# Moving weight splits, prepared sums and decoding units between VectorE and GpSimd in a planned attention and expert kernel

## The chip, the cores and the metric

The kernel runs on one core of a Trainium2 chip. Its time is the device time of one execution in microseconds (us). A core has TensorE (PE in the profile; its weight loads are PEld), VectorE (DVE), ScalarE (ACT), GpSimd (POOL) and SyncE (SP), which here issues every DMA. Each engine works through its own instructions strictly in the order of the program and waits on semaphores for the others. DVE, ACT and POOL work on SBUF; matmuls write PSUM, which DVE and ACT read.

## The reference

Three layers follow one another; only shapes and formulas matter here.

```
attention: B,H,S,D = 2,8,768,64; state = gamma[h]*state + k_t v_t ; y_t = scale * q_t state
experts:   x = attention as (1536, 512); P = softmax-like weights (1536, 8), 8 rounds of row and column scaling
           out = sum over e of P[:, e] * (relu(x @ w1[e]) @ w2[e]),   w1 (8,512,1024), w2 (8,1024,512)
last:      h = x @ w_in (512,2048); g = max(h,0) + alpha*min(h,0); out = g @ w_out (2048,512)
```

w_in, w_out and alpha come in as 64-bit numbers; the kernel turns w_in and w_out into 32-bit ones itself ("decoding").

## The kernel before

After the attention (the first 64 us) the work is 20 phases. Phases 0 to 7 are the eight experts on batch 0, phases 8 to 15 the same experts on batch 1 ("fast" in the code), phases 16 to 19 the last layer, two for each batch. A phase takes four weight units j = 0 to 3; weight unit n is 4 x phase + j.

**Split numbers.** Each 32-bit operand is split into a high part, rounded by ACT, and a low part, the difference, made by DVE or POOL. A product is three matmuls (high x high, high x low, low x high; lines 195 to 197).

**Layer 1** uses seven products of half blocks for each unit (Strassen-Winograd), six matmuls of 384 columns each. The list `order` has the 28 products of a phase; places 0 to 27 below mean "after that product". Unit 3 has its products (3,1), (3,5), (3,6), (3,2), (3,7) at places 19, 20, 22, 24 and 25, with products of unit 2 at 21 and 23. After product 6 DVE adds PSUM tile B and tile d into tile E (L700), and product 7 then goes on accumulating in B. So PE may not start product 7 of a unit before DVE has read B. For unit 0 there is one product between 6 and 7 (places 2 and 4), for the others there are two (8 and 11, 15 and 18, 22 and 25). After product 7 DVE adds again (L713, tile D). DVE makes the low halves hl of the layer's output (L656).

**Layer 2** of phases 0 to 7 and 16 to 19 is plain: six token tiles t0 to t5, 24 matmuls of 512 columns each; places 28 to 39 are t0a, t0, t1a, ... t5 (half a tile each). In phases 8 to 15 it is seven-product work again, 28 steps u at places 28 to 55, with weight pieces that phases 0 to 7 prepared and stored in DRAM (c2).

**Work beside the products** is put by hand at places, by `step(ph, pos, fn)`; what stands at one place goes to each engine in the order of registration:
- w1 units (L106 sums, L126 high, L135 low; tiles raw0, wa, wb, wc).
- w2 high (L145) and low (L150; tiles raw1, v). In phases 1 to 7 units 0 and 1 have their low part on DVE, units 2 and 3 on POOL, each in one instruction of 1024 columns.
- "prepared" units (`prep_at`: load, four sums L177, high L181, two low halves L185, two stores; tiles pr, pw): five a phase in phases 1 to 6, two in phase 7. The sums of one a phase are on DVE, of the others on POOL.
- decoding units (`decode_at`: load, `bits` = L593, L595, L598 on DVE, `power` = L603 on ACT, `join` = L609, L612 on DVE, store and the next load): 32 in all, 18 before phase 8 and two in each of phases 8 to 14. The load of the next unit is issued with the store of the last, into one buffer.
- in phases 10 to 15, `gather` (L826 on POOL) adds the eight weighted tiles t of the phase before to the total.

Of the kernel before, what the change touches and what calls it, by code (L numbers as in the profile page):

```python
# [44 lines left out]
def tile_kernel(ctx, tc, qkT, kv, ctab, w_gate, w1, w2, w_in, w_out, alpha, out):  # L45
# [31 lines left out]
    def w_load(kind, n):  # L77
        if n >= NJ * len(PHASES) or (kind, n) in raw:
            return
        ph, j = divmod(n, NJ)  # L80
        _, e = PHASES[ph]
        if kind == 1 and ph in FAST:
            return
        width = (1792, 1024)[kind]
        t = (stg, pools["raw1"])[kind].tile([128, width], F32, tag=f"raw{kind}", name=f"raw{kind}_{n}")
        src = (w1, w2)[kind][NJ * e + j] if e < E else wd[kind][NJ * (e - E) + j]
        if ph in FAST:
            nc.sync.dma_start(out=t[:, 0:768], in_=src[:, 0:768])
# [73 lines left out]
    def prep_load(i):  # L162
        if i >= NJ * E:
            return
        q = 2 if i == NJ * E - 1 else i % 3
        pr[i] = (pools["prep"] if q == 2 else tmp).tile([128, 1024], F32, tag="u" + "abc"[q], name=f"pr{i}")
        nc.sync.dma_start(out=pr[i], in_=w2[i])

    def prep_sums(i, eng, part):
        s11, s21, s12, s22 = (pr[i][:, 256 * q:256 * q + 256] for q in range(4))  # L170
        for out, in0, in1, op in (
            (s22, s21, s22, ALU.add),
            (s21, s11, s21, ALU.subtract),
            (s11, s22, s11, ALU.subtract),
            (s12, s12, s11, ALU.subtract),
        )[part]:
            eng.tensor_tensor(out=out, in0=in0, in1=in1, op=op)  # L177
# [113 lines left out]
    with tc.manual_schedule():  # L291
# [605 lines left out]
        def at(ph, key, *fns):  # L897
            hooks.setdefault((ph, key), []).extend(fns)
# [41 lines left out]
        for ph in range(len(PHASES)):  # L940
            n = NJ * ph
            fast = ph in FAST
            eng = dve if fast else pool
            if 1 <= ph <= 6:
                if ph > 1:
                    decode_at(ph, 15, 17, 19, 21)
                for i in (30, 36):
                    decode_at(ph, i, i + 1, i + 2, i + 3)
                prep_at(ph, dve, 9, 13, 16, (20, 23), 26)
                for q in (25, 30, 33, 36):  # L950
                    h = max(q, 27)
                    prep_at(ph, pool, q, q, h + 2, (h + 3, h + 3), h + 4)
            elif ph == 7:
                decode_at(ph, 15, 17, 19, 21)
                prep_at(ph, dve, 9, 13, 16, (20, 23), 26)
                prep_at(ph, pool, 25, 25, 30, (31, 31), 33)
            if fast:
                w1_at(ph, n + 2, pool, dve, 0, 2, 3, 3, 5, 7, 9)
                w1_at(ph, n + 3, pool, dve, 5, 9, 11, 10, 12, 14, 16)
                w1_at(ph, n + 4, pool, dve, 36, 36, 38, 39, 40, 42, 43)  # L960
                w1_at(ph, n + 5, pool, dve, 44, 44, 45, 48, 49, 50, 52)
            else:
                w1_at(ph, n + 2, pool, pool, 0, 3, 3, 6, 6, 9, 9)
                w1_at(ph, n + 3, pool, pool, 5, 10, 10, 12, 12, 16, 16)
                if ph > 0:
                    w1_at(ph, n + 4, dve, dve, 29, 29, 30, 31, 32, 31, 32)
                    w1_at(ph, n + 5, dve, dve, 33, 33, 34, 35, 36, 35, 36)
                early = ((4, 6, dve), (9, 12, dve), (15, 16, pool), (20, 21, pool))
                usual = ((12, 12, pool), (17, 17, pool), (19, 19, pool), (23, 23, pool))
                for j, (hi, lo, eng) in enumerate(early if 0 < ph < E else usual):  # L970
                    step(ph, hi, lambda m=n + j: w2_high(m))
                    step(ph, lo, lambda m=n + j, eng=eng: w2_low(m, eng))
                if ph < E:
                    for j, pos in enumerate((19, 22, 29, 31)):
                        step(ph, pos, lambda m=n + j: w2_keep(m))
            if fast:
                if ph < 2 * E - 1:
                    decode_at(ph, 5, 7, *((8, 9) if ph == E else (9, 11)))
                    decode_at(ph, 19, 21, 23, 25)
                if ph > E + 1:  # L980
# [12 lines left out]
                if ph in (E + 1, E + 4):
                    step(ph, 0, lambda k=(ph - E - 1) // 3: xk.extend(x_keep(2, k)))
                if E < ph < 2 * E - 1:
                    for keys in ((12, 17, 18, 27), (37, 39, 41, 45), (46, 48, 50, 55)):
                        i = unit[0] - NJ * E
                        if i >= 7 * ((ph - E - 1) // 3 + 1):
                            continue
                        unit[0] += 1  # L1000
                        for q, pos in enumerate(keys):
                            step(ph, pos, lambda i=i, q=q: xk[i][q]())
            if ph + 1 in XGROUP:
                g = XGROUP[ph + 1]
# [139 lines left out]
```

## Time and profile before

| | us |
|---|---|
| median of 3 runs | 1328.22 (1328.04 to 1329.6) |
| the profiled execution's own time | 1330.52 |
| its span | 1328.7 |
| PE busy | 1289.4 (97%) |
| DVE busy | 958.7 (72%) |
| ACT busy | 634.7 (48%) |
| POOL busy | 518.9 (39%) |

The span is the time from the first to the last instruction; 1.8 us of the execution lie around it. A busy share is an average over stages with different limits; matmuls overlap one another, so a busy PE is not a PE at full rate. The groups below name a line of the kernel before, an engine, and tiles as output<-inputs.

### The profile page before, as it was taken

The numbers are of one execution on the slowest core, as the hardware profiler recorded it, in microseconds if no ns is written. First come the engines' busy times: TensorE is split into PE (matmuls) and PEld (weight loads), VectorE is DVE, ScalarE is ACT, GpSimd is POOL, SyncE is SP. The second block draws the span as 40 slices with busy tenths as digits, with TensorE's granted clock in tenths as the row PEclk, the third lists the DMA queues.
The fourth block names the chain that finished last, engine by engine and source line by source line (L and its number), as shares of the span: only waits on it lengthen the run. The fifth ranks groups of instructions, "written<-read, shape, count | busy, mean of one in ns | idle before, by whom it ended". The sixth has DMA issues, their size and how long they took to land.

```text
span 1328.7 us, 19564 instructions
## 1 busy us (share of the span) xinstructions
PE 1289.4 (97%) x7179; PEld 1195.4 (90%) x7179; DVE 958.7 (72%) x1462; ACT 634.7 (48%) x1129; POOL 518.9 (39%) x435
## 2 busy tenths in 40 slices
PE   9899999999898989899999999999999999999998
PEld 6798988888888888888999999999999998989897
DVE  5646787888888787965878878797886775586371
ACT  2452625252626252544455646455564654646370
POOL 4860656464747473700004040322402272525160
PEclk9999999999999999999999999999999999999999
DMA  9464798888888888976768586776857572243111
GB/s 362 169 200 146 225 298 292 282 296 292 284 304 298 282 297 278 313 243 216 242 211 300 190 278 210 268 237 226 295 171 253 178 273 82 68 137 105 55 32 48
DMA packets 152255, 296.80 MB, mean 223 GB/s; under 512 B 11952, under 2 KB 77024, under 8 KB 152160
## 3 DMA queue, kind: packets, MB, share of 16 engines
q1 hardware_dynamic: 152160, 295.57, 66.1%
q8 instruction: 56, 0.92, 0.3%
q14 instruction: 39, 0.32, 0.1%
HBM read 198.24 MB, written 97.28 MB: 222 GB/s over the span
## 4 chain that ended last, share of the span: by engine, by line
PE 69%; DVE 12%; DMA 5%; issue 5%; ACT 5%; POOL 2%; SPq 2%; DVEq 0%; ACTq 0%; POOLq 0%
PE o L195 7%; PE o L197 7%; PE o L196 7%; PE B L195 7%; PE B L197 7%; PE B L196 7%; PE A L195 4%; PE A L197 4%; PE A L196 4%; PE D L196 2%; PE D L195 2%; PE D L197 2%; PE E L196 2%; PE E L195 2%; PE E L197 2%
## 5 line engine op out<-in xcount | busy, mean ns | idle before, releaser
L177 POOL TENSOR_TENSOR pr<-pr 128x256 f32<-128x256 f32 x100 | 97.9, 979 | 138.7 <-DMA pr<-in_w_dram 113.3
L106 POOL TENSOR_TENSOR raw<-raw 128x256 f32<-128x256 f32 x108 | 95.1, 891 | 92.7 <-DMA raw<-in_w_dram 24.4
L784 ACT ACTIVATE hs<-b 128x768 fp32r<-128x768 f32 x112 | 93.9, 846 | 32.5 <-PE A L197 11.4
L826 POOL TENSOR_TENSOR total<-total,t 128x384 f32<-128x384 f32 x56 | 66.3, 1212 | 103.2 <-DVE t L822 103.1
L794 DVE TENSOR_TENSOR hs<-b,hs 128x768 fp32r<-128x768 f32 x96 | 92.6, 972 | 14.8 <-ACT hs L784 14.8
L700 DVE TENSOR_TENSOR E<-B,d 128x384 f32<-128x384 f32 x80 | 45.1, 563 | 69.3 <-PE B L197 64.3
L697 ACT ACTIVATE B<-A 128x384 f32<-128x384 f32 x80 | 38.8, 485 | 104.8 <-PE A L197 103.0
L259 POOL TENSOR_TENSOR xs<-b,xs 128x384 fp32r<-128x384 f32 x6 | 6.2, 1025 | 199.4 <-DMA rd<-in_w_in_dram 120.9
L181 ACT ACTIVATE pw<-pr 128x1024 fp32r<-128x1024 f32 x32 | 33.8, 1056 | 82.1 <-POOL pr L177 79.4
L197 PE MATMUL B<-hs,ws 128*128 128x384 f32 x192 | 64.2, 334 | 0.0
L195 PE MATMUL B<-hs,ws 128*128 128x384 f32 x192 | 64.1, 334 | 0.0
L196 PE MATMUL B<-hs,ws 128*128 128x384 f32 x192 | 64.1, 334 | 0.0
L748 DVE SCALAR_TENSOR_TENSOR total<-o,P,total 128x512 f32<-128x512 f32 x42 | 31.3, 746 | 42.9 <-PE o L197 42.9
L185 DVE TENSOR_TENSOR pr<-pr,pw 128x512 fp32r<-128x512 f32 x64 | 60.1, 971 | 0.0
L603 ACT ACTIVATE ex<-ex,ebias 128x512 uint32<-128x512 uint32 x32 | 23.0, 718 | 65.6 <-DVE ex L593 65.6
L106 DVE TENSOR_TENSOR raw<-raw 128x256 f32<-128x256 f32 x84 | 50.1, 614 | 1.9 <-DMA raw<-in_w_dram 0.5
L713 DVE TENSOR_TENSOR D<-B,d 128x384 f32<-128x384 f32 x48 | 26.9, 561 | 23.2 <-PE B L197 23.1
L742 ACT ACTIVATE total<-o 128x512 f32<-128x512 f32 x18 | 10.8, 599 | 68.7 <-PE o L197 68.7
L195 PE MATMUL A<-hs,ws 128*128 128x384 f32 x128 | 42.9, 335 | 0.0
L196 PE MATMUL A<-hs,ws 128*128 128x384 f32 x128 | 42.8, 335 | 0.0
L197 PE MATMUL A<-hs,ws 128*128 128x384 f32 x128 | 42.8, 335 | 0.0
L692 ACT ACTIVATE d<-D 128x384 f32<-128x384 f32 x64 | 31.3, 489 | 15.1 <-PE D L197 15.1
(3435 smaller groups left out, 4722.3 us busy)
## 6 DMA issues: line engine op xcount, KB each, us to landing
ws<-c SPq DMA_DIRECT2D x112, 512.0 KB, 5.1
raw<-in_w_dram SPq DMA_DIRECT2D x64, 512.0 KB, 4.9
c<-raw SPq DMA_DIRECT2D x32, 512.0 KB, 6.6
pr<-in_w_dram SPq DMA_DIRECT2D x32, 512.0 KB, 5.8
c<-pw SPq DMA_DIRECT2D x32, 512.0 KB, 6.7
c<-pr SPq DMA_DIRECT2D x32, 512.0 KB, 7.2
raw<-c SPq DMA_DIRECT2D x32, 512.0 KB, 6.0
raw<-wd SPq DMA_DIRECT2D x32, 512.0 KB, 3.7
```

The lines of the kernel that those rows point to most:

```text
L106: eng.tensor_tensor(out=out, in0=in0, in1=in1, op=op)
L177: eng.tensor_tensor(out=out, in0=in0, in1=in1, op=op)
L181: nc.scalar.activation(out=ph2[i], in_=pr[i], func=AF.Copy)
L185: nc.vector.tensor_tensor(out=pr[i][:, a].bitcast(F32R), in0=pr[i][:, a], in1=ph2[i][:, a].bitcast(F32), op=ALU.subtract)
L195: nc.tensor.matmul(ps, ah, bh, start=first, stop=False, skip_group_check=True)
L196: nc.tensor.matmul(ps, ah, bl, start=False, stop=False, skip_group_check=True)
L197: nc.tensor.matmul(ps, alo, bh, start=False, stop=last, skip_group_check=True)
L697: nc.scalar.activation(out=banks[n, "B"], in_=banks[n, "A"], func=AF.Copy)
L700: nc.vector.tensor_tensor(out=banks[n, "E"], in0=banks[n, "B"], in1=banks[n, "d"], op=add)
L784: nc.scalar.activation(out=t[:, 0, :], in_=hsource(ph, k), func=func)
L794: nc.vector.tensor_tensor(out=lo, in0=src, in1=hi.bitcast(F32), op=ALU.subtract)
L826: nc.gpsimd.tensor_tensor(out=dst, in0=dst, in1=tt[m, h], op=ALU.add)
```

## The change

The low part of a w2 unit is made in two instructions of 512 columns instead of one of 1024 (in every plain phase). In phases 1 to 7 all eight of them are on DVE. The sums of prepared units in phases 1 to 6 are three on DVE and two on POOL (one and four before). Decoding has nine units before phase 8 (two in phase 0, one in each of 1 to 7) and 23 in phases 8 to 15: three in each of 8 to 14, two in 15. The third unit of a fast phase has its `bits` at place 53 and its `join` at place 60, which is place 0 of the next phase. Some w1 low parts of fast phases, and the transposes of phase 8, stand at other places.

```diff
-    def w2_low(n, eng):
-        hi, lo = (t.rearrange("p a b -> p (a b)") for t in ws2[n])
-        eng.tensor_tensor(out=lo, in0=raw[1, n], in1=hi.bitcast(F32), op=ALU.subtract)
-        w_load(1, n + 2)
+    def w2_low(n, q, eng):
+        hi, lo = (t[:, q, :] for t in ws2[n])
+        eng.tensor_tensor(out=lo, in0=raw[1, n][:, 512 * q:512 * q + 512], in1=hi.bitcast(F32), op=ALU.subtract)
+        if q == 1:
+            w_load(1, n + 2)
...
+            if pos >= 60:
+                ph, pos = ph + 1, pos - 60
...
-            if 1 <= ph <= 6:
-                if ph > 1:
-                    decode_at(ph, 15, 17, 19, 21)
-                for i in (30, 36):
-                    decode_at(ph, i, i + 1, i + 2, i + 3)
-                prep_at(ph, dve, 9, 13, 16, (20, 23), 26)
-                for q in (25, 30, 33, 36):
-                    h = max(q, 27)
-                    prep_at(ph, pool, q, q, h + 2, (h + 3, h + 3), h + 4)
...
+            if ph == 0:
+                decode_at(ph, 9, 11, 13, 14)
+                decode_at(ph, 21, 23, 25, 26)
+            elif ph < E:
+                decode_at(ph, *((32, 34, 36, 37) if ph < 7 else (15, 17, 19, 21)))
+                prep_at(ph, dve, 9, 14, 9, 17, 20, 21, 26)
+                prep_at(ph, pool, 25, 25, 25, 29, 30, 30, 31)
+                if ph < 7:
+                    prep_at(ph, dve, 31, 31, 31, 33, 34, 34, 35)
+                    prep_at(ph, dve, 35, 35, 34, 37, 38, 38, 39)
+                    prep_at(ph, pool, 37, 37, 37, 39, 61, 61, 63)
...
-                early = ((4, 6, dve), (9, 12, dve), (15, 16, pool), (20, 21, pool))
+                early = ((4, 6, 7, dve), (9, 12, 13, dve), (15, 16, 19, dve), (22, 23, 24, dve))
...
+                decode_at(ph, *((11, 13, 14, 16) if ph == E else (9, 11, 12, 13)))
+                decode_at(ph, *((22, 24, 26, 27) if ph == E else (20, 22, 23, 25)))
                 if ph < 2 * E - 1:
-                    decode_at(ph, 5, 7, *((8, 9) if ph == E else (9, 11)))
-                    decode_at(ph, 19, 21, 23, 25)
+                    decode_at(ph, 53, 55, 60, 61)
...
-        for a, (key, later) in enumerate(zip(("t3", "t4", "t4", "t5"), (order[i] for i in (0, 1, 13, 14)))):
+        for a, (key, later) in enumerate(zip(("t3", "t4", "t4", "t5"), (order[i] for i in (0, 1, 5, 6)))):
```

The numbers of `prep_at` are now: sums, sums, load of the next, high, low, low, store. New line numbers are one higher from L150 on.

The first place is DVE in phase 2, from the add after product 7 of unit 2 (D10) to the add after product 6 of unit 3 (E11). Before:

```order
L713 TENSOR_TENSOR D10_2406<-B10_2395,d10_2413 128x384
L656 SCALAR_TENSOR_TENSOR hl10_00_2470<-A10_2388,hh10_00_2469 128x384
L656 SCALAR_TENSOR_TENSOR hl10_11_2482<-D10_2406,hh10_11_2481 128x384
L609 SCALAR_TENSOR_TENSOR a0_1_0_2437<-a0_1_0_2437,ex0_1_0_2435 128x512
L612 SCALAR_TENSOR_TENSOR a0_1_0_2437<-rd0_1_0_2229,a0_1_0_2437 128x512
L185 TENSOR_TENSOR pr5_2172<-pr5_2172,pw5_2452 128x512
L700 TENSOR_TENSOR E11_2535<-B11_2492,d11_2508 128x384
```

And on DVE in the changed kernel, from the same add to the same add:

```order
L714 TENSOR_TENSOR D10_2424<-B10_2415,d10_2431 128x384
L657 SCALAR_TENSOR_TENSOR hl10_00_2482<-A10_2408,hh10_00_2481 128x384
L657 SCALAR_TENSOR_TENSOR hl10_11_2495<-D10_2424,hh10_11_2494 128x384
L150 TENSOR_TENSOR v10l_2457<-raw1_10_2350,v10h_2456 128x512
L186 TENSOR_TENSOR pr5_2216<-pr5_2216,pw5_2485 128x512 x2
L701 TENSOR_TENSOR E11_2541<-B11_2505,d11_2522 128x384
```

The two instructions of a decoding unit's join are gone from this stretch; one half of v10l has come in, and both low halves of the prepared unit stand ahead of the add instead of one.

The second place is POOL in phase 2, from the last w1 low part (wb11l) to the first w1 sums for the next phase. Before:

```order
L135 TENSOR_TENSOR wb11l_2455<-raw0_11_2180,wb11h_2454 128x512
L150 TENSOR_TENSOR v10l_2441<-raw1_10_2321,v10h_2440 128x1024
L150 TENSOR_TENSOR v11l_2512<-raw1_11_2404,v11h_2511 128x1024
L177 TENSOR_TENSOR pr6_2350<-pr6_2350 128x256 x4
L177 TENSOR_TENSOR pr7_2573<-pr7_2573 128x256 x4
L177 TENSOR_TENSOR pr8_2662<-pr8_2662 128x256 x4
L177 TENSOR_TENSOR pr9_2734<-pr9_2734 128x256 x4
L106 TENSOR_TENSOR raw0_14_2714<-raw0_14_2714 128x256 x4
```

And on POOL in the changed kernel, over the same stretch:

```order
L135 TENSOR_TENSOR wb11l_2469<-raw0_11_2192,wb11h_2468 128x512
L178 TENSOR_TENSOR pr6_2372<-pr6_2372 128x256 x4
L178 TENSOR_TENSOR pr9_2762<-pr9_2762 128x256 x4
L106 TENSOR_TENSOR raw0_14_2721<-raw0_14_2721 128x256 x4
```

Two instructions of 1024 columns and the sums of two prepared units have left POOL.

The third place is DVE at the end of phase 10 and the start of phase 11, from the last w1 low part of phase 10 (wb45l) to the first add of phase 11 (E44). Before:

```order
L135 TENSOR_TENSOR wb45l_7847<-raw0_45_7477,wb45h_7846 128x512
L822 TENSOR_TENSOR t10_20_7885<-B2_10_0_7619,pb10_7297 128x384
L822 TENSOR_TENSOR t10_30_7895<-B2_10_1_7630,pb10_7297 128x384
L700 TENSOR_TENSOR E44_7926<-B44_7905,d44_7916 128x384
L135 TENSOR_TENSOR wa46l_7929<-raw0_46_7767,wa46h_7928 128x512
```

And on DVE in the changed kernel:

```order
L135 TENSOR_TENSOR wb45l_7802<-raw0_45_7432,wb45h_7801 128x512
L594 TENSOR_SCALAR ex0_4_1_7834<-rd0_4_1_7527 128x512
L596 TENSOR_SCALAR a0_4_1_7836<-rd0_4_1_7527 128x512
L599 SCALAR_TENSOR_TENSOR a0_4_1_7836<-rd0_4_1_7527,a0_4_1_7836 128x512
L823 TENSOR_TENSOR t10_20_7845<-B2_10_0_7574,pb10_7249 128x384
L823 TENSOR_TENSOR t10_30_7855<-B2_10_1_7585,pb10_7249 128x384
L610 SCALAR_TENSOR_TENSOR a0_4_1_7836<-a0_4_1_7836,ex0_4_1_7834 128x512
L613 SCALAR_TENSOR_TENSOR a0_4_1_7836<-rd0_4_1_7527,a0_4_1_7836 128x512
L701 TENSOR_TENSOR E44_7892<-B44_7866,d44_7879 128x384
```

The five instructions of the third decoding unit stand between wb45l and E44, three ahead of the weighted tiles t and two behind them.

## Rows read from the trace of the kernel before

**Rows 1.** Stretches: us, busy us (instructions) by engine, granted PE clock, DMA share, GB/s.
```profile
129.30:192.40 63.10, 62.43 (x317) 56.43 (x316) 47.28 (x67) 31.26 (x54) 33.48 (x28) 1.00 0.79 257
192.40:530.60 338.20, 319.42 (x1562) 286.55 (x1561) 274.94 (x377) 143.26 (x241) 193.13 (x162) 0.98 0.86 292
530.60:600.10 69.50, 65.76 (x326) 58.64 (x324) 51.68 (x78) 33.00 (x61) 27.31 (x20) 0.98 0.80 266
600.10:664.20 64.10, 60.59 (x350) 59.49 (x349) 44.55 (x64) 32.83 (x57) 0.00 (x0) 1.00 0.71 237
722.70:1073.00 350.30, 350.30 (x2017) 349.65 (x2017) 274.80 (x374) 188.45 (x321) 86.25 (x75) 1.00 0.71 238
223.00:226.00 3.00, 2.83 (x11) 2.84 (x12) 2.98 (x6) 0.45 (x1) 2.02 (x3) 0.69 0.89 267
```

**Rows 2.** Waits: engine line waited for: us in total, times, longest us.
```profile
PE B L195 <- DVE E L700: 25.7, 15, 2.8
```

**Rows 3.** Timeline of PE, phase 2: start us, us, instruction, idle before and its releaser.
```profile
220.09 0.34 PE L197 MATMUL A<-xh,wa11l 128*128 128x384 f32 x1
223.17 0.45 PE L195 MATMUL B<-xh,wc11h 128*128 128x384 f32 x1 [2.73 <-DVE E L700]
```

**Rows 4.** Timeline of DVE, same stretch of phase 2.
```profile
216.62 2.09 DVE L609 SCALAR_TENSOR_TENSOR a<-a,ex 128x512 f32<-128x512 f32 x1
218.75 2.76 DVE L612 SCALAR_TENSOR_TENSOR a<-rd,a 128x512 uint32<-128x512 uint32 x1
221.43 1.21 DVE L185 TENSOR_TENSOR pr<-pr,pw 128x512 fp32r<-128x512 f32 x1
222.56 0.55 DVE L700 TENSOR_TENSOR E<-B,d 128x384 f32<-128x384 f32 x1
```

**Rows 5.** Timeline of POOL, same stretch of phase 2.
```profile
218.13 2.83 POOL L150 TENSOR_TENSOR v11l<-raw,v11h 128x1024 fp32r<-128x1024 f32 x1
220.92 4.25 POOL L177 TENSOR_TENSOR pr<-pr 128x256 f32<-128x256 f32 x4
```

**Rows 6.** Single lines, whole run: duration ns min/median/max, first and last start us.
```profile
L185 DVE TENSOR_TENSOR pr<-pr,pw x64: 674/1054/2396, 151.8 to 579.7; 128x512 fp32r<-128x512 f32 x64
L609 DVE SCALAR_TENSOR_TENSOR a<-a,ex x32: 674/692/2098, 173.5 to 981.1; 128x512 f32<-128x512 f32 x32
L593 DVE TENSOR_SCALAR ex<-rd x32: 414/422/962, 169.1 to 976.9; 128x512 uint32<-128x512 uint32 x32
```

**Rows 7.** Timelines of POOL and DVE in phase 5, before product 7 of unit 2.
```profile
410.89 2.51 POOL L135 TENSOR_TENSOR wc23l<-raw,wc23h 128x768 fp32r<-128x768 f32 x1 [0.29 <-ACT wc23h L126]
...
410.18 1.50 DVE L150 TENSOR_TENSOR v21l<-raw,v21h 128x1024 fp32r<-128x1024 f32 x1
411.60 2.53 DVE L177 TENSOR_TENSOR pr<-pr 128x256 f32<-128x256 f32 x2
414.05 0.56 DVE L700 TENSOR_TENSOR E<-B,d 128x384 f32<-128x384 f32 x1
```

**Rows 8.** Timeline of DVE in phase 8.
```profile
627.22 0.43 DVE L593 TENSOR_SCALAR ex<-rd 128x512 uint32<-128x512 uint32 x1 [3.10 <-DMA xd<-tt]
```

**Rows 9.** DMA issues from 652 to 1010 us: count, KB each, median us to landing.
```profile
rd<-in_w_out_dram SPq DMA_DIRECT2D x8, 512.0 KB, 5.2
```

**Rows 10.** Timelines of DVE, POOL and PE where phase 10 ends and 11 begins.
```profile
778.75 1.04 DVE L135 TENSOR_TENSOR wb45l<-raw,wb45h 128x512 fp32r<-128x512 f32 x1
780.34 0.56 DVE L822 TENSOR_TENSOR t<-B,pb 128x384 f32<-128x384 f32 x1 [0.54 <-PE B L197]
781.38 0.56 DVE L822 TENSOR_TENSOR t<-B,pb 128x384 f32<-128x384 f32 x1 [0.49 <-PE B L197]
784.60 0.57 DVE L700 TENSOR_TENSOR E<-B,d 128x384 f32<-128x384 f32 x1 [2.66 <-PE B L197]
...
777.59 7.94 POOL L826 TENSOR_TENSOR total<-total,t 128x384 f32<-128x384 f32 x7 [3.77 <-DVE t L822]
...
785.37 0.34 PE L195 MATMUL B<-xh,wc44h 128*128 128x384 f32 x1
```

More of the change, by code (lines that the diff above doesn't have):

```diff
@@ L921, in tile_kernel, with prep_at @@
         unit = [0]
-        def prep_at(ph, eng, s0, s1, hi, lo, st):
+        def prep_at(ph, eng, s0, s1, ld, hi, l0, l1, st):
             i = unit[0]
             unit[0] += 1
-            step(ph, s0, lambda: prep_load(i + 1), lambda: prep_sums(i, eng, slice(0, 2)))
+            step(ph, s0, lambda: prep_sums(i, eng, slice(0, 2)))
             step(ph, s1, lambda: prep_sums(i, eng, slice(2, 4)))
+            step(ph, ld, lambda: prep_load(i + 1))
             step(ph, hi, lambda: prep_high(i))
-            for q, pos in enumerate(lo):
-                step(ph, pos, lambda q=q: prep_low(i, q))
-            step(*(ph, st) if st < 40 else (ph + 1, st - 40), lambda: prep_store(i))
+            step(ph, l0, lambda: prep_low(i, 0))
+            step(ph, l1, lambda: prep_low(i, 1))
+            step(ph, st, lambda: prep_store(i))
         def w1_at(ph, m, add_eng, eng, adds, ah, al, ch, cl, bh, bl):
@@ L943, in tile_kernel @@
             eng = dve if fast else pool
-            if 1 <= ph <= 6:
-                if ph > 1:
-                    decode_at(ph, 15, 17, 19, 21)
-                for i in (30, 36):
-                    decode_at(ph, i, i + 1, i + 2, i + 3)
-                prep_at(ph, dve, 9, 13, 16, (20, 23), 26)
-                for q in (25, 30, 33, 36):
-                    h = max(q, 27)
-                    prep_at(ph, pool, q, q, h + 2, (h + 3, h + 3), h + 4)
[L953 to L956, printed above, removed]
+            if ph == 0:
[9 more added lines that the diff above has]
+                    prep_at(ph, pool, 37, 37, 37, 39, 61, 61, 63)
             if fast:
-                w1_at(ph, n + 2, pool, dve, 0, 2, 3, 3, 5, 7, 9)
-                w1_at(ph, n + 3, pool, dve, 5, 9, 11, 10, 12, 14, 16)
+                w1_at(ph, n + 2, pool, dve, 0, 2, 3, 3, 5, 5, 7)
+                w1_at(ph, n + 3, pool, dve, 5, 9, 14, 10, 15, 12, 16)
                 w1_at(ph, n + 4, pool, dve, 36, 36, 38, 39, 40, 42, 43)
@@ L967, in tile_kernel @@
                     w1_at(ph, n + 5, dve, dve, 33, 33, 34, 35, 36, 35, 36)
-                early = ((4, 6, dve), (9, 12, dve), (15, 16, pool), (20, 21, pool))
-                usual = ((12, 12, pool), (17, 17, pool), (19, 19, pool), (23, 23, pool))
-                for j, (hi, lo, eng) in enumerate(early if 0 < ph < E else usual):
+                early = ((4, 6, 7, dve), (9, 12, 13, dve), (15, 16, 19, dve), (22, 23, 24, dve))
+                usual = ((12, 12, 12, pool), (17, 17, 17, pool), (19, 19, 19, pool), (23, 23, 23, pool))
+                for j, (hi, l0, l1, eng) in enumerate(early if 0 < ph < E else usual):
                     step(ph, hi, lambda m=n + j: w2_high(m))
-                    step(ph, lo, lambda m=n + j, eng=eng: w2_low(m, eng))
+                    step(ph, l0, lambda m=n + j, eng=eng: w2_low(m, 0, eng))
+                    step(ph, l1, lambda m=n + j, eng=eng: w2_low(m, 1, eng))
                 if ph < E:
@@ L1015, in tile_kernel @@
         assert not todo and unit[0] == NJ * E + 14
-        at(0, "t5", lambda: decode_load((0, 0, 0)), lambda: prep_load(0))
+        at(0, (0, 5), lambda: decode_load((0, 0, 0)))
+        at(0, "t5", lambda: prep_load(0))
         for w in range(6):
             at(E, ((0, 7), (1, 5), (1, 6), (1, 2), (2, 1), (2, 6))[w], lambda w=w: ws_load(E, w))
-        for a, (key, later) in enumerate(zip(("t3", "t4", "t4", "t5"), (order[i] for i in (0, 1, 13, 14)))):
+        for a, (key, later) in enumerate(zip(("t3", "t4", "t4", "t5"), (order[i] for i in (0, 1, 5, 6)))):
             at(E - 1, key, lambda a=a: turn(2, a, 0))
```

## The prediction

> **What bounds the kernel now.** I read the stretches by phase first, cut at the first matmul of each phase. A phase of layer 1 and plain layer 2 has the same matmuls in phases 1 to 6. Phase 1 takes 63.1 us, phases 2 to 6 together 338.2 us, 67.6 each [rows 1]; phase 7 takes 69.5 and phase 8 64.1, while phases 10 to 15 take 350.3, 58.4 each, with PE busy for every microsecond. So the bound is PE's rate, and what can be won lies in phases 2 to 8: phases 9 to 15 have nothing to give, and can only lose.
>
> The waits come next. PE's one large wait is for DVE's add E<-B,d at L700: 25.7 us in 15 pieces, the longest 2.8 [rows 2]. The timeline shows one of them: in phase 2 PE starts its last matmul of product 2 of unit 3 at 220.09 and stands 2.73 us until 223.17 [rows 3]. It waited for the add at 222.56, and ahead of the add DVE's queue holds the join of a decoding unit, 2.09 and 2.76 us, and a low half of 1.21 [rows 4]. It is long because POOL works beside it on low parts of 1024 columns, v11l for 2.83 us, and then on prepared sums [rows 5]; in the median of the run the first of the two takes 0.69 [rows 6]. [...]
>
> What the rows show is that DVE instructions with two SBUF inputs and POOL's instructions take turns. [...]
>
> **Phases 2 to 6.** Phase 1 is the model: it has no decoding unit ahead of that add, and it has its 63.1 us with two low parts of 1024 columns still on POOL. The change takes the join out of this stretch in phases 2 to 6. What stands there instead is half of v10l and both low halves of the prepared unit. From 216.62, when the join began [rows 4], three instructions of 0.68 end at 218.7 (starts lie a little closer than that). With POOL in between each is about 1.21, as the L185 in [rows 4], and they end at 220.2; the add then ends about 220.8. PE would go on at 220.09 + 0.17 = 220.3, so what is left of 2.73 us is 0 to 0.5. The 2.4 us worst of L185 [rows 6] needs a POOL instruction of 1024 columns, and none is left there. DVE trades per phase: two decoding units less (each two instructions as L593, 0.42, and three as L609, 0.69: 2.9 us), and four pieces of 0.68 and eight sums of half that width more: 5.8 against 5.4 us. So DVE is no more loaded, and POOL loses two instructions of up to 2.83 and eight of 1.06 (4.25 for four), about 13 us a phase [rows 5]. The wait at product 7 of unit 2 stays: in phase 5 wc23l on POOL holds two sums for 2.53 us, and the add comes at 414.05 [rows 7]; the order there is unchanged, and phase 1 has this wait in its 63.1 too. The term is 5 x 63.1 = 315.5 against 338.2, **-22.7 us**. Bounds: at best PE never stands still, 62.4 a phase (its busy time in phase 1), -26; at worst half is given back to waits like those of unit 2, -11.
>
> **Phase 7** keeps its decoding at places 15 to 21 and gets a piece and both low halves there as well: five contended instructions of 0.68 to 1.21 in place of three. They end 0 to 2.2 us after the add is due; middle 1.1, where 2.7 were lost, and a shorter wait spares the stretch at the lower clock. **-3.0 us**, bounds 0 and -6.4 (69.5 - 63.1).
>
> **Phase 8.** The `bits` at place 19 waited 3.10 us for the store xd<-tt of a transposed block, whose buffer they use [rows 8]. The transposes move from places 13 and 14 to 5 and 6, and the `bits` to 11 and 22, so five products lie between them, 5.2 us (six matmuls of 350.3/2017 = 0.174 us each make 1.04). 64.1 - 58.4 = 5.7 us are over; 14 more matmuls than 336 stay, at most 2.4. **-4.0 us**, bounds -3.3 and -5.7.
>
> **Phase 0** gets two units; the second `bits` comes seven products, 7.3 us, behind the store that issues its load, and a load lands 5.2 us after its issue [rows 9]. **+0.4**, bounds 0 and 2. In phases 16 to 19 and 0 the two pieces stay on POOL and are ready long before layer 2: 0.
>
> **Phases 10 to 15.** Their `bits` at 9 and 20 stand seven products or more behind their load, which takes 5.2 us [rows 9]: no wait. Not covered is the third unit. Before E44, DVE has idle gaps of 0.54, 0.49 and 2.66 [rows 10]; the five instructions are 2.9 us. They would fit if alone. But POOL is in seven gathers for 7.94 us from 777.59, 1.1 each [rows 10], and L593 goes up to 0.96, L609 up to 2.10 beside POOL [rows 6]. Going through the queue, with a wait of 0.6 to 0.95 behind a gather: wb45l ends 779.7; L594 waits to 780.65 and ends 781.0; L596 waits to 782.0 and ends 782.3; L599 ends 782.95; the two tiles t, from PSUM and unhindered, come by 783.9, so the gathers that need them come later too; L610 ends about 785.05, L613 786.6. The add then starts near 786.55, not 784.60, and ends 1.95 later than its 785.17. PE's product 7 is due at 785.37 [rows 10], so PE loses about 1.7 at the start of each of the six phases that have gathers (phase 9 has none): 6 x 1.7 = **+10.2 us**. Bounds: 0 if nothing waits; at the worst rows, 0.96 twice, 2.10 twice and 2.76 make 8.9, less 3.7 of gaps 5.2, and a lowered clock behind it, 0.31 x 3 = 0.9 as in phase 2.
>
> **Sum.** -22.7 - 3.0 - 4.0 + 0.4 + 10.2 = -19.1. From the profiled execution's 1330.5 that gives 1311.4; that execution stands 2.3 above the median of 1328.2, so the median I predict is **1309 us**.
>
> **Rivals.**
> 1. *The third unit is hidden.* If DVE gets its turns without a full wait, as in the median rows (L593 0.42, L609 0.69), 2.9 us fit into 3.7 of gaps. For it: the fast phases lose nothing today. Against it: wb45l, in the same place, takes 1.04 where others of its size take 0.68 [rows 6, 10]. Then -29.3: 1299 us.
> 2. *The pieces wait.* Each piece of 512 on DVE must find its own turn. In phase 5 the low part went through in 1.50 and wc23l came behind it [rows 7]; cut in two, wc23l can go between the pieces, and another POOL instruction between the sums. The wait ahead of product 7 of unit 2 then grows by about 1.7 (a wc low of 2.51 less the part it waits itself) in six phases, 10 us: 1319 us. For it: the strict turns in [rows 4, 5]. Against it: POOL has 12 us less to do. [...]
> 3. *Slower: the third unit stops PE longer than the old join did.* At its worst rows that is 5.2 + 0.9 = 6.1 us in each of six phases, 36.6 in all. It decides the sign from 29.3 / 6 = 4.9 us a phase on; at 6.1 the sum is +7.3: 1335 us. For it: 2.76 has been seen behind POOL. Against it: those were instructions of 1024 columns, and a gather takes 1.1.
> 4. *No difference*, gains and losses by chance within 0.2%: it needs 29 us of new losses, nothing in the rows points at this number.
>
> **How the numbers follow.** Forecast 0.48 (its own range 1303 to 1314), rival 1 0.22, rival 2 0.22, rival 3 0.05, rival 4 0.03. About 0.2%, 2.7 us, is what can be told from no change. Faster takes the first three, 0.92; same 0.03; slower 0.05. The range from 1294 to 1322 holds the forecast and rivals 1 and 2 with some room for the bounds of phases 2 to 6, and leaves out the two last.
>
> **What would show it.** Right, if in the profile after phases 2 to 6 take about 63 us each, the add before product 7 of unit 3 has no PE wait over 0.5 us and the granted clock stays at full speed there; if phase 8 takes about 60; and if phases 10 to 15 take about 60 instead of 58.4, with one PE wait of 1 to 2 us each behind E<-B,d of their unit 0, and L594, L596, L610 and L613 near 1 us there. Wrong, if those six phases still take 58.4 (rival 1), if waits before product 7 of unit 2 go beyond 2 us (rival 2), if PE waits for a decoding load, or if new waits of PE name another engine than DVE.

## The result, and the profile after

The changed kernel takes 1341.31 us (median of 4 runs, 1340.84 to 1342.66), the kernel before 1328.91 beside it: ratio 1.0092, interval 1.0074 to 1.0109. It is 0.9% slower, clear of the interval, where 1309 had been forecast. The profiled execution has a span of 1338.9 us, 10.2 more than before.

The stretches by phase of the changed kernel, columns as in [rows 1]: phase 0, 1, 2 to 6, 7, 8, 9, and 10 to 15.

```profile
63.90:137.10 73.20, 68.63 (x336) 60.92 (x337) 45.56 (x129) 26.62 (x48) 27.60 (x26) 0.95 0.56 180
137.10:200.20 63.10, 62.44 (x317) 56.47 (x316) 46.51 (x78) 31.98 (x54) 23.26 (x21) 1.00 0.79 254
200.20:514.70 314.50, 310.90 (x1561) 280.66 (x1560) 242.06 (x395) 138.51 (x230) 119.32 (x111) 1.00 0.89 288
514.70:581.90 67.20, 64.32 (x325) 57.19 (x325) 49.58 (x82) 32.30 (x60) 18.02 (x16) 1.00 0.78 259
581.90:647.50 65.60, 62.21 (x351) 61.12 (x350) 45.87 (x67) 33.11 (x58) 0.00 (x0) 0.97 0.68 232
647.50:708.60 61.10, 59.45 (x337) 58.16 (x337) 49.75 (x67) 31.75 (x56) 12.15 (x9) 1.00 0.74 240
708.60:1083.00 374.40, 357.77 (x2018) 348.78 (x2018) 314.52 (x414) 190.94 (x329) 100.37 (x75) 1.00 0.72 240
```

| phases | before, us | after, us | difference | forecast |
|---|---|---|---|---|
| 0 | 65.4 | 73.2 | +7.8 | +0.4 |
| 2 to 6 | 338.2 | 314.6 | -23.6 | -22.7 |
| 7 | 69.5 | 67.2 | -2.3 | -3.0 |
| 8 | 64.1 | 65.6 | +1.4 | -4.0 |
| 9 | 58.5 | 61.1 | +2.6 | 0 |
| 10 to 15 | 350.3 | 374.4 | +24.1 | +10.2 |
| 16 to 19 | 251.4 | 252.1 | +0.7 | 0 |

(Differences are of unrounded starts of the phases, first matmul to first matmul, and for the last row to the end of the last matmul; phase 1 is unchanged at 63.1. They add up to +10.7.) The gain came as forecast and was lost elsewhere. PE's waits for the add E grew from 15 to 31 in number [rows 2]; the row has us in total, times and the longest:

```profile
PE B L196 <- DVE E L701: 28.3, 31, 4.4
```

**Where the gain is.** In phase 2 the stretch of [rows 3 to 5] now reads, first a matmul of PE's product 7 of unit 3, which has no wait in its row, then DVE ahead of the add, then POOL:

```profile
227.17 0.34 PE L196 MATMUL B<-xh,wc11h 128*128 128x384 f32 x1
...
222.99 0.81 DVE L150 TENSOR_TENSOR v10l<-raw,v10h 128x512 fp32r<-128x512 f32 x1
223.73 1.83 DVE L186 TENSOR_TENSOR pr<-pr,pw 128x512 fp32r<-128x512 f32 x2
225.48 0.55 DVE L701 TENSOR_TENSOR E<-B,d 128x384 f32<-128x384 f32 x1
...
220.42 3.99 POOL L178 TENSOR_TENSOR pr<-pr 128x256 f32<-128x256 f32 x4
```

The three instructions ahead of the add last 0.81 and 1.83 (for two) beside POOL, and the add ends at 226.0, 1.1 us before PE reaches that product.

**The start of phase 11**, which answers to [rows 10], on DVE, POOL and PE:

```profile
769.91 1.23 DVE L594 TENSOR_SCALAR ex<-rd 128x512 uint32<-128x512 uint32 x1
771.06 1.24 DVE L596 TENSOR_SCALAR a<-rd 128x512 uint32<-128x512 uint32 x1
...
773.88 1.26 DVE L610 SCALAR_TENSOR_TENSOR a<-a,ex 128x512 f32<-128x512 f32 x1
775.17 1.38 DVE L613 SCALAR_TENSOR_TENSOR a<-rd,a 128x512 uint32<-128x512 uint32 x1
776.48 0.55 DVE L701 TENSOR_TENSOR E<-B,d 128x384 f32<-128x384 f32 x1
...
773.58 5.25 POOL L827 TENSOR_TENSOR total<-total,t 128x384 f32<-128x384 f32 x4 [1.56 <-DVE t L823]
...
777.08 0.44 PE L196 MATMUL B<-xh,wc44h 128*128 128x384 f32 x1 [1.37 <-DVE E L701]
```

This is what had been forecast: four of the third unit's five instructions take 1.2 to 1.4 us each beside the gathers, and PE stands 1.37 us. A gap is counted here against PE's pace of 0.17 us from one matmul's start to the next, which makes it 0.16 more than the idle time in the row. Over the six phases the gap there is 0.8 or 1.5 us, 7.8 in all.

**What had not been forecast** comes seven products later, before product (1,7), in the rows of PE, ACT and DVE:

```profile
783.11 0.34 PE L197 MATMUL E<-xl,wb44h 128*128 128x384 f32 x1
...
783.54 0.63 ACT L126 ACTIVATE wb46h<-raw 128x512 fp32r<-128x512 f32 x1 [3.57 <-PE E L197]
784.08 0.47 ACT L693 ACTIVATE d<-D 128x384 f32<-128x384 f32 x1
...
784.21 0.69 DVE L135 TENSOR_TENSOR wb46l<-raw,wb46h 128x512 fp32r<-128x512 f32 x1 [4.04 <-ACT wb46h L126]
784.81 0.56 DVE L701 TENSOR_TENSOR E<-B,d 128x384 f32<-128x384 f32 x1
...
785.43 0.45 PE L196 MATMUL B<-xh,wc45h 128*128 128x384 f32 x1 [0.77 <-DVE E L701]
```

Part b of a w1 unit has two buffers, taken in turn. wb46h needs the one of wb44h, which PE reads last in product (0,3), at place 9. The change moved the high of wb46 from place 7 to 5 and its low from 9 to 7. (The section on the change speaks of low parts alone, and its diff leaves these lines out; two highs moved too.) So ACT stands 3.57 us in front of it, the tile d of unit 1 (place 6), which is now behind it, is late, DVE stands 4.04 us for the low part, and the add behind that is late. The same happens to unit n+3 (high of b from 14 to 12, now ahead of d at 13). In each of phases 9 to 14 PE's gaps are 0.93 before product (1,7), 0.65 before (2,7) and 0.4 before (2,4), and in most of them another 0.4 before (3,4).

**Phase 0**, on SP, DVE and PE:

```profile
86.36 0.33 SPq L91 DMA_DIRECT2D raw<-in_w_dram  x1
86.74 0.42 SPq L618 DMA_DIRECT2D wd<-a  x1
87.20 0.43 SPq L584 DMA_DIRECT2D rd<-in_w_in_dram  x1
...
81.43 0.69 DVE L613 SCALAR_TENSOR_TENSOR a<-rd,a 128x512 uint32<-128x512 uint32 x1
...
93.97 0.62 DVE L594 TENSOR_SCALAR ex<-rd 128x512 uint32<-128x512 uint32 x1 [6.68 <-DMA rd<-in_w_in_dram]
...
96.17 0.69 PE L196 MATMUL B<-xh,wc3h 128*128 128x384 f32 x1 [4.37 <-DVE E L701]
```

The first unit's join ends at 82.1, but its store is issued at 86.74: SP stood before L91, the load of a w2 unit that waits for v0l on POOL (to 86.3). The next load goes out at 87.20 and has landed by 93.9, 6.7 us later. DVE stands 6.68 us in front of the `bits`, the add of unit 3 stands behind them, and PE waits 4.37. After this wait the granted clock is 0.50 and the matmuls start 0.32 us apart until 101.5, where they started 0.17 apart before it; from these spacings I estimate about 2.5 us more. Here are the two us from 98 on:

```profile
98.00:100.00 2.00, 2.00 (x8) 2.00 (x7) 1.50 (x3) 0.49 (x1) 2.00 (x2) 0.50 1.09 382
```

**Phase 8**, which answers to [rows 8], on ACT, DVE and PE:

```profile
593.84 0.63 ACT L126 ACTIVATE wb34h<-raw 128x512 fp32r<-128x512 f32 x1 [4.18 <-PE E L197]
594.38 0.47 ACT L892 ACTIVATE tt<-tr 128x384 f32<-128x384 f32 x1
...
602.27 0.63 ACT L126 ACTIVATE wb35h<-raw 128x512 fp32r<-128x512 f32 x1 [3.15 <-PE E L197]
...
603.18 0.71 ACT L604 ACTIVATE ex<-ex,ebias 128x512 uint32<-128x512 uint32 x1
...
600.11 0.43 DVE L596 TENSOR_SCALAR a<-rd 128x512 uint32<-128x512 uint32 x1 [1.97 <-DMA xd<-tt]
...
603.92 0.69 DVE L610 SCALAR_TENSOR_TENSOR a<-a,ex 128x512 f32<-128x512 f32 x1 [1.18 <-ACT ex L604]
...
605.87 0.45 PE L196 MATMUL B<-xh,wc34h 128*128 128x384 f32 x1 [2.42 <-DVE E L701]
```

The copies of the transposed blocks now stand behind wb34h, which waits 4.18 us; so their store is late and the `bits` still wait 1.97 us for it. That is not what PE pays for. The unit's `power` (L604, place 13) stands on ACT behind wb35h (place 12), which waits 3.15 us for its buffer; the join waits for the `power`, the add behind the join is late, and PE stands 2.42 us before product (2,7). Another gap of 1.0 before (1,7) is that of wb34h, as in the later phases.

### The profile page after: what moved, and what is told of

Its sections match the earlier page's. It is cut to its first block, busy times and chain, and to the rows that moved or that the text cites. A ratio compares the mean times of both kernels' runs of the same rounds, so it can differ in the third digit from the quotient of the medians.

```text
span 1338.9 us, 19554 instructions
## 1 busy us (share of the span) xinstructions
PE 1293.1 (97%) x7179; PEld 1191.4 (89%) x7179; DVE 973.0 (73%) x1552; ACT 634.0 (47%) x1129; POOL 444.1 (33%) x393
## 3 DMA queue, kind: packets, MB, share of 16 engines
q1 hardware_dynamic: 152160, 295.57, 66.6%
## 4 chain that ended last, share of the span: by engine, by line
PE 75%; DVE 10%; DMA 4%; POOL 4%; issue 3%; ACT 3%; SPq 0%; DVEq 0%; POOLq 0%; ACTq 0%
PE o L196 10%; PE o L198 10%; PE o L197 10%; PE B L196 7%; PE B L198 6%; PE B L197 6%; PE A L196 4%; PE A L198 4%; PE A L197 4%; PE D L197 2%; PE D L198 2%; PE D L196 2%; PE E L197 2%; PE E L196 2%; PE E L198 2%
## 5 line engine op out<-in xcount | busy, mean ns | idle before, releaser
L106 POOL TENSOR_TENSOR raw<-raw 128x256 f32<-128x256 f32 x108 | 91.7, 859 | 96.6 <-DMA raw<-wd 42.9
L178 POOL TENSOR_TENSOR pr<-pr 128x256 f32<-128x256 f32 x52 | 51.6, 992 | 197.8 <-DMA pr<-in_w_dram 162.6
L827 POOL TENSOR_TENSOR total<-total,t 128x384 f32<-128x384 f32 x56 | 75.6, 1375 | 113.0 <-DVE t L823 112.9
L260 POOL TENSOR_TENSOR xs<-b,xs 128x384 fp32r<-128x384 f32 x6 | 7.9, 1311 | 207.9 <-ACT xs L256 207.9
L698 ACT ACTIVATE B<-A 128x384 f32<-128x384 f32 x80 | 38.6, 483 | 58.3 <-PE A L198 56.5
L604 ACT ACTIVATE ex<-ex,ebias 128x512 uint32<-128x512 uint32 x32 | 22.9, 715 | 60.0 <-DVE ex L594 60.0
L186 DVE TENSOR_TENSOR pr<-pr,pw 128x512 fp32r<-128x512 f32 x64 | 49.6, 815 | 0.0
L178 DVE TENSOR_TENSOR pr<-pr 128x256 f32<-128x256 f32 x76 | 45.5, 598 | 1.7
L106 DVE TENSOR_TENSOR raw<-raw 128x256 f32<-128x256 f32 x84 | 36.9, 457 | 1.4
```

The lines of the kernel that those rows point to most:

```text
L186: nc.vector.tensor_tensor(out=pr[i][:, a].bitcast(F32R), in0=pr[i][:, a], in1=ph2[i][:, a].bitcast(F32), op=ALU.subtract)
L698: nc.scalar.activation(out=banks[n, "B"], in_=banks[n, "A"], func=AF.Copy)
L827: nc.gpsimd.tensor_tensor(out=dst, in0=dst, in1=tt[m, h], op=ALU.add)
```

## The experiments

Runs e1 to e4, e5 to e8 and e9 to e11 have each set its own runs of the kernel before, on one chip. Ratios are to these; the span in brackets is the interval. The medians of the kernel before are 1331.8, 1331.5 and 1332.9 us in the three sets and 1328.9 beside the changed kernel, so times of different sets are compared by their ratios or by stretches of their traces.

**e1: the w1 places alone undone.**

```diff
-                w1_at(ph, n + 2, pool, dve, 0, 2, 3, 3, 5, 5, 7)
-                w1_at(ph, n + 3, pool, dve, 5, 9, 14, 10, 15, 12, 16)
+                w1_at(ph, n + 2, pool, dve, 0, 2, 3, 3, 5, 7, 9)
+                w1_at(ph, n + 3, pool, dve, 5, 9, 11, 10, 12, 14, 16)
```

> The changed kernel with the old places of the w1 splits in the fast phases (high of part b at 7 and 14 again, not at 5 and 12). Theory W (the buffer): at place 5 ACT's high part of unit n+2 must wait until product (0,3) at place 9 has read the tile it overwrites; ACT stands, so its copy d of place 6 and DVE's add come late. Then the PE waits of 0.93 and 0.65 us before products (1,7) and (2,7), and the 0.39 behind them, go in phases 9 to 15 (2.3 to 2.6 us each, 18 in all), and 3 to 5 us of phase 8: 1341.3 - 22 = 1319 us. Theory Q (the third decoding unit loads DVE too much): those waits stay, 1341. In both the waits at the start of phases 10 to 15 (0.8 to 1.5) stay.

Measured: 1321.25 us, 0.9918 (0.9899 to 0.9937). Two lines turn a slower kernel into a faster one. wb46h now waits 1.35 us instead of 3.57, d stands ahead of it again, and nothing on PE waits for it; phase 8 takes 61.5 instead of 65.6, phases 10 to 15 take 360.7 instead of 374.4:

```profile
773.77 0.63 ACT L126 ACTIVATE wb46h<-raw 128x512 fp32r<-128x512 f32 x1 [1.35 <-PE E L197]
...
580.50:642.00 61.50, 60.24 (x351) 59.51 (x349) 45.66 (x67) 33.75 (x58) 0.00 (x0) 1.00 0.75 246
701.40:1062.10 360.70, 352.78 (x2017) 349.27 (x2017) 312.16 (x414) 194.28 (x329) 96.34 (x75) 1.00 0.74 249
```

**e2: the w1 places alone, in the kernel before** (the same two lines the other way).

> The kernel before with one part of the change alone, the new places of the w1 splits in the fast phases; decoding stays two units a phase. Theory W: the same waits of 0.9 and 0.65 us appear in phases 8 to 15 without a third unit, 2.3 to 2.6 us each: 1328.9 + 19 = 1348 us. Theory Q: without the third unit nothing happens, 1329 us.

Measured: 1350.17 us, 1.0138 (1.0117 to 1.0159). Phases 9 to 14 take 60.8 to 61.2 instead of 58.4, with the same gaps of 0.93, 0.65 and 0.4 and no decoding changed. Theory W holds there. In phase 8 it does not: that phase takes 61.6 instead of 64.1, less than before. Its `power` stands at 7 and 21 in this kernel, not at 13 behind wb35h; so what phase 8 loses in the changed kernel is the new w1 places together with the new decoding places.

**e9: of these places only part b of unit n+2 undone.**

```diff
-                w1_at(ph, n + 2, pool, dve, 0, 2, 3, 3, 5, 5, 7)
+                w1_at(ph, n + 2, pool, dve, 0, 2, 3, 3, 5, 7, 9)
```

> The changed kernel with one w1 part alone back at its old place: the high of part b of unit n+2 in the fast phases at 7 and its low at 9, all else as changed. Theory B (a part b has two buffers; at place 5 its high on ACT must wait until PE has read the buffer in product (0,3) at 9, and what stands behind it on ACT comes late): the wait of 0.93 us before product (1,7) goes in phases 9 to 15, the one of 0.65 before (2,7), which is that of unit n+3's part b, and the two of 0.4 stay; 7 x 0.93 = 6.5 us less than the changed kernel, 1335 us. Theory L (DVE has too many low parts in too few places): the 0.93 comes back a few products later, phases 9 to 15 keep 62 to 62.8, 1341 us.

Measured: 1333.19 us, 1.0002 (0.9989 to 1.0015). The 0.93 is gone in phases 9 to 15, the 0.65 and the 0.4 stay; in the stretch of phase 11 wb46h waits 1.35 us and wb47h, unit n+3's, still 2.58 and holds d behind it:

```profile
780.61 0.63 ACT L126 ACTIVATE wb46h<-raw 128x512 fp32r<-128x512 f32 x1 [1.35 <-PE E L197]
...
787.89 0.63 ACT L126 ACTIVATE wb47h<-raw 128x512 fp32r<-128x512 f32 x1 [2.58 <-PE E L197]
788.42 0.47 ACT L693 ACTIVATE d<-D 128x384 f32<-128x384 f32 x1
...
605.09 0.44 PE L196 MATMUL B<-xh,wc34h 128*128 128x384 f32 x1 [2.42 <-DVE E L701]
```

Theory B holds for this part; the 0.93 did not come back elsewhere, as theory L had it. High and low moved together, so their shares are not told apart. The last line is of phase 8: wb34h is back at its place there, the `bits` wait for no store, and PE's 2.42 us stay, so they are wb35h's. That a third buffer would do the same was not tried.

**e3: phase 0's second unit in its layer 2.**

```diff
-                decode_at(ph, 21, 23, 25, 26)
+                decode_at(ph, 29, 31, 33, 34)
```

> The changed kernel with the second decoding unit of phase 0 at places 29, 31, 33, 34 and not 21, 23, 25, 26. Theory S (SP's queue): the load of that unit is issued late, behind a raw load that waits for the low part v0l on POOL, and lands 7 us after its place; DVE stands for it ahead of the add of unit 3, PE waits 4.5 us and then runs at a lower clock. Later places take it away: phase 0 from 73.2 to about 65.6 us, 1341.3 - 7.6 = 1334 us. Theory P (POOL's work in pieces slows DVE there): phase 0 stays near 73, 1341 us.

Measured: 1336.33 us, 1.0030 (1.0014 to 1.0045). Phase 0 takes 68.9 us instead of 73.2, not the 65.6 of theory S; the long wait is gone, 1.2 before product (3,7) and 0.9 in layer 2 remain.

**e4: the third unit of a fast phase earlier in layer 2.**

```diff
-                    decode_at(ph, 53, 55, 60, 61)
+                    decode_at(ph, 45, 47, 49, 50)
```

> The changed kernel with the third decoding unit of the fast phases at places 45, 47, 49, 50 and not 53, 55, 60, 61: the same work, ahead of the gathers and not across the start of the next phase. Theory G (gathers and the unit take turns ahead of the first add): the waits of 1.53 and 0.82 us at the start of phases 10 to 15 go, 7.8 us: 1333.5 us; those before products (1,7) and (2,7) stay. Theory Q (DVE has no room for a third unit): the time is lost at another place of the phase, 1341 us.

Measured: 1347.97 us, 1.0119 (1.0102 to 1.0136). The waits at the start of phases 10 to 15 are gone, but phases 9 to 14 have a new one of 0.9 to 2.1 us, 60 to 62 us in, before a layer-2 matmul whose low part hs is late on DVE. Theory G's 1333.5 missed; the time is lost at another place, as theory Q had it, and more of it. PE and DVE in phase 10:

```profile
772.62 0.45 PE L197 MATMUL B<-hs,ws 128*128 128x384 f32 x1 [1.96 <-DVE hs L795]
...
769.83 0.68 DVE L610 SCALAR_TENSOR_TENSOR a<-a,ex 128x512 f32<-128x512 f32 x1
770.54 0.69 DVE L613 SCALAR_TENSOR_TENSOR a<-rd,a 128x512 uint32<-128x512 uint32 x1
...
771.62 0.95 DVE L795 TENSOR_TENSOR hs<-b,hs 128x768 fp32r<-128x768 f32 x1
```

**e5: e1 and e3 together, and the third unit's join behind the first add** (53, 55, 63, 64; the other two units at 11, 13, 14, 15 and 21, 23, 24, 25).

> The changed kernel with the w1 parts of the fast phases at their old places, the second unit of phase 0 in layer 2 (both as measured singly before), and the third unit's join at place 3 of the next phase, behind the first add, and its store at 4; the first unit of each fast phase follows later, bits at 11. Theory A (what stops PE at the start of phases 10 to 15 is the join in front of the add while POOL is in its gathers): without it the six waits of 0.8 to 1.5 us go, phases 10 to 15 take 58.8 instead of 60, and the time is 1321 (w1 places alone) - 4.3 (phase 0: 73.2 to 68.9) - 7.5 = 1309 us. Theory Q (DVE has no room for a third unit in a fast phase, wherever it stands, as with the third unit at 45 to 50): the start waits go, others of the same sum come at products (1,7) or in layer 2, phases 10 to 15 stay at 60 or more, 1317 us.

Measured: 1335.64 us, 1.0032 (1.0014 to 1.0050). Both theories miss (1309 and 1317). The start waits are gone, but phases 10 to 15 take 61 to 65: the second unit, one place later than in the changed kernel, now has its `power` behind ACT's high of hs, its join waits for that, and PE waits 1.80 us for the add behind the join:

```profile
789.27 0.69 DVE L610 SCALAR_TENSOR_TENSOR a<-a,ex 128x512 f32<-128x512 f32 x1 [1.43 <-ACT ex L604]
791.48 0.55 DVE L709 TENSOR_TENSOR b<-B,d 128x384 f32<-128x384 f32 x1
...
792.08 0.45 PE L196 MATMUL B<-xh,wb47h 128*128 128x384 f32 x1 [1.80 <-DVE b L709]
```

**e11: as e5, but the other units at 10, 12, 13, 14 and 20, 22, 23, 25.**

> As the kernel with the third unit's join behind the first add, but the first unit's bits stand at 10 and the second unit's four places at 20, 22, 23, 25 as in the changed kernel. In that kernel the second unit, one place later, had its join wait 1.43 us for ACT beside the layer-2 highs, and PE stood 1.8 to 2 us there. Theory S (only that shift gave the time back): the waits of 2 us go, phases 10 to 14 take 59 to 59.6, 1321 - 4.3 - 5 = 1312 us. Theory Q (the third unit's 2.9 us of DVE work have no room in a fast phase): phases 10 to 15 stay at 61 or more, 1325 to 1335 us.

Measured: 1315.89 us, 0.9862 (0.9843 to 0.9882). The waits of 2 us are gone; phases 10 to 12 take 59.0 to 59.6, 13 and 14 still 61.1 and 60.4. One place of the other two units is worth about 20 us (1335.64 - 1315.89 = 19.8, of two sets; phases 9 to 15 take 440.3 and 417.7 in the two traces), so a third unit does find room in most phases, at the price of up to 0.8 us before product (0,4). Theory Q falls; S is met within 4 us.

**e6: e1 and e3, and no third unit in phases 9 to 14;** six units in layer 2 of phases 1 to 6 instead.

```diff
-                if ph < 2 * E - 1:
+                if ph == E:
                     decode_at(ph, 53, 55, 60, 61)
...
+                if ph < 7:
+                    decode_at(ph, 28, 29, 30, 31)
+                    decode_at(ph, 34, 35, 37, 38)
```

> As the last one, but no third unit in phases 9 to 14; the six units stand in layer 2 of phases 1 to 6 instead, two in each (bits at 28 and 34). Theory A (DVE is free for 1 to 4 us of 6 in layer 2 of phases 1 to 6 with POOL idle, so a second unit is hidden there): phases 1 to 6 stay at 62.8 and phases 10 to 15 go back to 58.4 to 58.8, 1321 - 4.3 - 6 x 1.5 = 1308 us. Theory D (the DMA share is 0.93 to 1.02 in that layer 2, so 0.75 MB more per phase push everything that is loaded there): up to 0.75 MB at 290 GB/s = 2.6 us in each of six phases come back, 1323 us, with PE waits on DMA or on w1 parts.

Measured: 1310.34 us, 0.9845 (0.9823 to 0.9868). Phases 2 to 6 stay at 62.7 to 62.8, phases 10 to 15 take 58.3 to 59.6. So theory A holds (1308), and the loads and stores that were added to those phases pushed nothing (theory D, 1323).

**e7: e1 with the low parts of w2 units 2 and 3 on POOL; e8: the kernel before with only the pieces on DVE.**

```diff
-                early = ((4, 6, 7, dve), (9, 12, 13, dve), (15, 16, 19, dve), (22, 23, 24, dve))
+                early = ((4, 6, 7, dve), (9, 12, 13, dve), (15, 16, 16, pool), (20, 21, 21, pool))
```

> The changed kernel with the w1 parts of the fast phases at their old places (1321 us) and the low parts of w2 units 2 and 3 on POOL again, at their old places, in two pieces of 512. Theory J (in phases 2 to 6 the decoding join in front of the add made the old wait): no wait comes back at (3,7), phases 2 to 6 stay at 62.8 to 63.1, as phase 1 of the kernel before with such low parts on POOL, 1321 us. Theory P (POOL's low parts beside DVE made it): the waits of 2.7 us come back, phases 2 to 6 take 66 to 67.6, 1337 to 1345 us.

> The kernel before with only the w2 low parts changed: all eight pieces on DVE at the new places; prepared sums and decoding units stay. Theory J (the join in front of the add): phases 2 to 6 keep most of their wait, since two pieces of 0.7 to 1.2 us now stand beside the join, 67 to 69 each, 1327 to 1335 us. Theory P (POOL's low parts of 1024 columns): without them the join runs in 0.7 per instruction, phases 2 to 6 take 63 to 64, 1305 to 1311 us.

Measured: e7 1322.91 us, 0.9944 (0.9927 to 0.9962); e8 1323.21 us, 0.9943 (0.9923 to 0.9962). Phases 2 to 6 of e7, then phases 2 to 6 of e8:

```profile
198.80:512.60 313.80, 310.48 (x1562) 280.78 (x1561) 226.10 (x375) 138.15 (x230) 141.11 (x131) 1.00 0.89 289
```

```profile
192.20:525.35 333.15, 315.97 (x1561) 281.58 (x1560) 278.45 (x407) 144.05 (x241) 166.78 (x152) 0.99 0.88 296
```

With the join gone and the pieces on POOL the whole gain is there (62.8 a phase); with the join in place and the pieces on DVE only 5 of 23.6 us are (66.6). So it is the decoding that left layer 1 which won phases 2 to 6. e7 keeps the new share of the prepared sums; phase 1 of the kernel before has the old share, and with no decoding in layer 1 it takes 63.1 [rows 1]. In e8 the join takes 0.78 and 0.69 us where it took 2.09 and 2.76 [rows 4], and the old wait before product (3,7) is gone too. But others stand in its place, 1.53 us in phase 2 behind the add D, after a `bits` instruction of 1.69 and a piece of 1.22. Theory P, which would have had 1305 to 1311, falls; J had 1327 to 1335 and is 4 us off. In phase 7, where the join still is, pieces on POOL cost: 69.8 in e7 against 67.6 in e1.

**e10: e6 without phase 0's two units and with phase 7's in layer 2; two units in layer 2 of phase 16.**

> The kernel without a third unit in phases 9 to 14 (1310 us), with phase 0's two decoding units and the one in layer 1 of phase 7 moved too: that of phase 7 to its layer 2 (bits at 28), two more units to layer 2 of phase 16 (bits at 28 and 34). Theory A (decoding costs nothing in a layer 2 where DVE is idle for part of every half tile): phase 0 goes from 68.8 to 65.5, as before with no unit, phase 7 from 67.1 to 65.2 or less with the join gone from its add, phase 16 stays at 63.2; 1310 - 3.3 - 1.9 = 1305 us. Rival: what phase 0 gains is lost in phase 16, or the wait in phase 7 is that of its other DVE work; 1309 to 1311 us.

Measured: 1304.05 us, 0.9775 (0.9755 to 0.9795), the fastest; theory A had 1305. Phase 0, phase 7, phases 10 to 15 and phase 16:

```profile
64.00:129.40 65.40, 65.40 (x337) 58.55 (x338) 38.21 (x119) 25.14 (x46) 26.89 (x26) 1.00 0.55 178
506.40:570.50 64.10, 63.44 (x326) 57.26 (x325) 49.26 (x82) 32.55 (x61) 19.99 (x18) 1.00 0.83 278
692.00:1046.20 354.20, 352.10 (x2018) 349.69 (x2017) 278.82 (x384) 190.01 (x323) 87.64 (x75) 1.00 0.73 241
1046.20:1109.20 63.00, 62.83 (x314) 55.97 (x313) 38.81 (x69) 32.87 (x59) 32.06 (x30) 1.00 0.46 151
```

Phase 0 is what it was before, phase 7 is 5.4 us shorter, and phase 16 pays nothing for its two units.

## Why the prediction was wrong, point by point

- **The step that failed is one that the prediction never took.** It costed the decoding units in phases 8 to 15 and put the w1 parts that move in the same phases at nothing, without a reason. That term is 15.4 us in phases 9 to 15 (changed kernel less e1: 435.5 less 420.1) and 4.1 in phase 8, together 19.4 before rounding, of the 29.8 us between the forecast sum of -19.1 and the +10.7 of the phases. e1 shows it by the time, e2 does for phases 9 to 15, and e9 shows the mechanism for its largest part. Another 7.4 us lie in phase 0.
- **Phases 2 to 6**, -22.7: right, -23.6. The reason was half right. The join had to go, as said, and POOL's low parts of 1024 columns did make it long (e8); that POOL lost them mattered little once the join was gone (e7). The size came from phase 1 as a whole, not from the one wait that was followed. That wait before (3,7) makes 14.6 of the 23.6; waits of 1.2 to 1.5 before product (0,7) of phases 2, 3 and 6 went too.
- **Phases 10 to 15**, 1.7 each from the third unit: the mechanism was right, by row; 0.8 or 1.5 at the start of each phase, 7.8 for the 10.2. With the old w1 places (e1) the six phases are 10.4 longer than before; that this meets 10.2 is in part luck, since only 7.8 of it is the wait that was forecast. Rival 3 is not what made it slower: no phase came near 6.1 us there, and its 0.9 for a lowered clock did not come: the granted clock over the six phases is 1.00. The time was lost in another place.
- **Phase 0**, +0.4, bounds 0 and 2: wrong, +7.8. The count of seven products took the store to be issued when the join ends. SP works in order, and the store stood 4.6 us behind a load that waited for POOL; then the load took 6.7 us and not 5.2 [rows 9]. e3 takes 4.3 of it back, e10 all.
- **Phase 8**, -4.0: wrong, +1.4. The distance between transposes and `bits` was right as far as it goes: with the old w1 places (e1) the `bits` wait for no store, and phase 8 takes 61.5, -2.6. With the new ones the copy of the transposed block stands on ACT behind wb34h, and the `power`, which PE pays for, behind wb35h.
- **Phase 7**, -3.0: -2.3. The wait before product (3,7) fell from 2.7 to 0.3 us, further than forecast; a new one of 1.7 stands before (2,4), behind the add D. The granted clock over the phase is 1.00, against 0.98 in [rows 1].
- **Rival 2**, the pieces wait: they do (one at 216.1 us in phase 2 takes 2.33 us, one with POOL idle 0.68), but PE did not pay for it. The gap before product (2,7) is 0.8 to 1.0 us in phases 1 to 6, as in phase 1 of before. Rival 1 falls by the start waits.
- **The chances.** Faster was given 0.92 because each edit that the prediction names was priced, and the bounds of the unknown were those of the priced edits alone. "If new waits of PE name another engine than DVE" was the wrong sign to watch: the new waits name DVE, and their cause sits on ACT, one releaser further back. The sign "if PE waits for a decoding load" did come, in phase 0.

What stays open: why phases 13 and 14 of e11 are 1 to 2 us longer than 10 to 12, why phase 8 of e2 is shorter than before, and how the 0.4 us late in layer 1 split between the moved lows of unit n+3.

## What to carry to other kernels

Price every moved instruction for the buffer that it writes, not only for its inputs: here wb46h, moved ahead of the last reader of its buffer's former tile, stood 3.57 us (1.35 in e1) for that reader, and d, which it had passed on ACT, was late with it, as was the `power` behind wb35h, which stood 3.15. Look for the room for extra work where the other engines' deadlines are slack (here a plain layer 2: with a second unit there, phases 2 to 6 of e6 stayed at 62.7 to 62.8 us), and follow each DMA through its issuing queue before you count on the time at which it starts (here a store stood 4.6 us). When a wait names an engine, go on to what that engine waited for.

## What was not expected of the hardware

DVE instructions with one SBUF input were held up beside POOL as well: L594 and L596 take 1.23 and 1.24 us beside the gathers, 0.42 without POOL, while the weighted tiles, whose first input is in PSUM, take 0.55 all through the run. The prediction's row [rows 6], of the first of these two instructions, had 0.96 as the worst; the second, L595 in the kernel before, took up to 1.23 there already, and the prediction has no row of it.

The same gaps of 0.93 and 0.65 us come back in each of phases 9 to 15. The next tile, wb46h, waits 3.57 us for its buffer there; but e9 takes the 0.93 us out of each of seven phases with the same two buffers, by order alone.
